# Stage four by sums and differences from batch 3 on, and a later exponential, in a prime-factor Fourier mixer with routed experts

## The chip, the cores and the metric

The kernel runs on one core of one Trainium2 chip. The metric is the device time of one execution in microseconds. The engines are named as the profile names them: PE (matrix products), PEld (its loads of the stationary operand), DVE (VectorE), ACT (ScalarE), POOL (GpSimd) and SP (SyncE, whose queue issues most DMAs).

## The reference

The first block multiplies the spectrum of each sequence with a filter; the second sends every token to one of eight experts.

```python
# x: (8, 2496, 256), filt: (1249, 256), N = 8 * 2496 tokens, E = 8, F = 1024
X = np.fft.rfft(x, axis=1)
y = np.fft.irfft(X * (filt_r + 1j * filt_i), n=2496, axis=1)
x = y.reshape(N, 256)
logits = x @ w_gate
expert_idx = np.argmax(logits, axis=1)
probs = np.exp(logits - logits.max(-1, keepdims=True))
probs /= probs.sum(-1, keepdims=True) + 1e-09
gate = probs[np.arange(N), expert_idx]
out[n] = gate[n] * (np.maximum(x[n] @ w1[e], 0) @ w2[e])     # e = expert_idx[n]
```

All data are float32. One expert per token, no token dropped.

## The kernel before

**The transform.** 2496 = 39 x 64, and a token is numbered by q (0 to 38) and t (0 to 63), so that the transform of length 2496 becomes one of 39 and one of 64. Because the input is real, 20 of the 39 frequencies are enough. A batch passes four stages on PE, each with a DRAM round trip between, except in batch 0: stage A (`stage_a`, L342) transforms over q, three values of t at a time: 3 x 39 = 117 rows in, 3 x 40 = 120 rows out, 20 frequencies as real and imaginary part. Stage B (`stage_b`, L356) transforms over t; DVE (in the first batches POOL too) multiplies with the filter (L363 to L372). Stage C (`stage_c`, L382) goes back over t and stores U (`ud`). **Stage four**, `stage_d`, goes back over q: 120 rows (3 t, 20 real and 20 imaginary parts each) times the table `tds` (120 x 117) give 117 rows of tokens, 3 t by 39 q. There are 22 columns of 3 t each; the last holds one t alone (63), so it has 40 rows in. They go in six chunks of four columns, the last chunk of two. `mm` on two columns at a time is L401 (120 rows, 512 output columns); in the last chunk it is L405, one column at a time, 120 rows and then 40.

**Around stage four.** `load_u` (L334) fetches a chunk of U into an input buffer `fin` (seven of them, shared with the other stages), by one DMA, two for the last chunk. `evac` copies a bank of PSUM to SBUF; the program decides by its own reckoning (`free`, `now`) whether DVE or ACT does it (L228). The result `yo` is the token rows themselves. `turn_y` transposes them (L476), `logits` multiplies by the gate's weights (L490: four groups of 32 output rows in one bank, one per pair of columns), `turn_logits` transposes back (L501). `route` then finds, for eight columns at a time, the expert and the gate: DVE instructions on small tiles, an exponential on ACT (L527), and the "rank product", two matmuls with a triangle and with ones (L548, L549), which count how many tokens of each expert come before. From it comes the row in a DRAM list by expert, and POOL writes each column's 117 token rows there by one indirect DMA (`scatter`, L617).

**The experts.** Tiles of 512, 256 or 128 rows of that list are read back (`rows_in`, L712), transposed (`turn_x`, L753, which first copies the token numbers to `idt`, L747), multiplied by the expert's w1 and w2, and written to the output by indirect DMAs that read `idt` (L860). Large tiles do the first product by a seven-product scheme of quarters (`hidden_by_quarters`, L796; sums on DVE, L800; relu on ACT, L804); others plainly (`hidden`, L837). The second product is `result` (L854).

**What sets the order.** The order on PE, DVE, ACT and SP is the order in which the Python program issues. A list of transform steps, each with a place in its slot (one slot per batch), a condition and a cost, is mixed with the steps of the experts: `share()` says how many microseconds of experts go with one of the transform; a step whose input has not been loaded, or whose landing time (`lands`) lies ahead, lets the experts go first. Side jobs (`sides`: routing, maps of tiles) are generators, advanced a few operations after each step. `free["v"]`, `free["s"]`, `free["p"]` are the program's reckoning of when DVE, ACT and POOL come free. In slot k stage four belongs to batch k - 1.

```python
            evac(yo[:, j:j + 2, :D], p[:TP, :].rearrange("p (i d) -> p i d", i=2), 512)
```

is L406, the end of stage four before: one copy of a bank for each pair of columns.

Of the kernel before, what the change touches and what calls it, by code (L numbers as in the profile page):

```python
# [19 lines left out]
P = 128  # L20
# [18 lines left out]

def token(q, t):  # L40
    return (q * N2 * pow(N2, -1, N1) + t * N1 * pow(N1, -1, N2)) % S


def coefficients():

    k = np.arange(S)
    of = np.zeros((N2, N1), int)
    of[k * pow(N1, -1, N2) % N2, k * pow(N2, -1, N1) % N1] = k
    return of[:, :NF]


def dft_tables():
# [27 lines left out]
    for j in range(NB):  # L80
# [6 lines left out]

    return {
# [6 lines left out]
        "valid": valid.reshape(TP, NG),  # L95
    }
# [22 lines left out]
def kernel(  # L119
# [13 lines left out]
    valid: bass.AP,  # L133
    out: bass.AP,
# [46 lines left out]

    tas = cst.tile([TP, TK], F32, name="tas")
    tbs = cst.tile([P, P], F32, name="tbs")
    tcs = cst.tile([P, P], F32, name="tcs")
    tds = cst.tile([TK, TP], F32, name="tds")
    sgs = cst.tile([P, NF // 2], F32, name="sgs")
# [5 lines left out]
    tri = cst.tile([TP, TP], F32, name="tri")  # L192
    ones = cst.tile([TP, P], F32, name="ones")
    segs = {w: cst.tile([P, E * w], F32, name=f"seg{w}") for w in (8, NG % 8)}
    ids0 = cst.tile([TP, NG], F32, name="ids0")
    vld = cst.tile([TP, NG], F32, name="vld")
# [63 lines left out]
    def load_rest():  # L260
        nc.sync.dma_start(out=tds, in_=td)
        nc.vector.memset(wg, 0.0)
        nc.sync.dma_start(out=wg[:, :, :E], in_=moe_w_gate.rearrange("(i p) e -> p i e", p=P))
        nc.sync.dma_start(out=ids0, in_=ids)
        nc.sync.dma_start(out=vld, in_=valid)

    def make_constants():
# [3 lines left out]
            out=tri, in_=ones[:, :TP], compare_op=ALU.is_gt, fill=0.0, base=0, pattern=[[1, TP]], channel_multiplier=-1  # L271
# [15 lines left out]
    def columns(ap, i0, n):  # L287
# [4 lines left out]
        if m < n:  # L292
            yield NS, slice(m, n), rows[(NG - 1) * TK:, :].rearrange("(i p) d -> p i d", p=NS)

# [35 lines left out]
    def load_u(b, c):  # L330
        i0, n = CH[c]
        ui = fin(("u", b, c))
        for r, m, v in columns(ud[b], i0, n):
            nc.sync.dma_start(out=ui[:r, m], in_=v)  # L334

    def stage_a(b, c):
        i0, n = CH[c]
        xt = ins.pop(("x", b, c))
        zo = sb.tile([TK, 4, D], F32, tag="st", name="zo", bufs=4)
        for j in range(0, n, 2):  # L340
            p = bank()
            mm(p[:TK, :], lhsT=tas, rhs=xt[:TP, j:j + 2, :], start=True, stop=True)  # L342
            evac(zo[:, j:j + 2, :], p[:TK, :].rearrange("p (t d) -> p t d", t=2), 512)
# [31 lines left out]
    def stage_c(b, f):  # L375
# [8 lines left out]
        if j == 2:  # L384
            f0 = f - 2
            move(ud[b][:, f0:f0 + 4, :], uo[:HP])
            move(ud[b][:, NF + f0:NF + f0 + 4, :], uo[HP:])
# [3 lines left out]
    def stage_d(b, c):  # L391
        if c == 0:
            lgs[b] = sb.tile([TP, NG, E], F32, tag="lg", name="lg")
# [3 lines left out]
        yo = outs["o", b, c] = sb.tile([P, 4, DR], F32, tag="y", name="yo", bufs=YB)[:TP]  # L397
        for j in range(0, n, 2):
            p = bank()
            if i0 + j + 2 < NG:  # L400
                mm(p[:TP, :], lhsT=tds, rhs=ui[:TK, j:j + 2, :], start=True, stop=True)  # L401
            else:

                for i, k in enumerate((TK, NS)):
                    mm(p[:TP, i * D:(i + 1) * D], lhsT=tds[:k, :], rhs=ui[:k, j + i, :], start=True, stop=True)  # L405
# [64 lines left out]
    def turn_y(b, c):  # L470
        yo = outs["o", b, c]
        for j in range(0, CH[c][1], 2):
            pt = bank().rearrange("p (i q) -> p i q", i=4)
            for i in range(2):
                for dh in range(DH):
                    nc.tensor.transpose(  # L476
                        pt[:, 2 * i + dh, :TP], yo[:, j + i, dh * P:(dh + 1) * P], ident[:TP, :TP]
                    )
            yt = yts[b, c, j] = sb.tile([P, 4, TP], F32, tag="yt", name="yt", bufs=4)
            evac(yt, pt[:, :, :TP], 4 * TP)  # L480

    def logits(b, g):
# [4 lines left out]
        lt = psr.tile([P, 2, E * NG], F32, tag="rk", name="lt")[:, :, :TP]  # L487
# [4 lines left out]
        ls = sb.tile([P, 2, TP], F32, tag="ls", name="ls", bufs=1)  # L492
# [3 lines left out]
    def turn_logits(b):  # L496
        g, w, ls = outs.pop(("l", b))
        n = w // CT
        pt = bank()[:TP, :2 * w].rearrange("p (i w) -> p i w", i=2)
# [8 lines left out]
    def route(b, g):  # L508
        t0 = 8 * g
        w = min(8, NG - t0)  # L510
        lg = lgs[b][:, t0:t0 + w]
        sh3 = (TP, w, E)
        she = (TP, E, w)

        def small(name, *shape, dt=F32, tag=None, rows=TP):
# [11 lines left out]
        nc.scalar.activation(ex, ex, AF.Exp)  # L527
        nc.vector.tensor_tensor(oh, oh, em8[:TP, None, :].to_broadcast(sh3), op=ALU.mult)
# [4 lines left out]
        nc.vector.tensor_tensor(idx, idx, vld[:, t0:t0 + w], op=ALU.mult)  # L533
# [3 lines left out]
            oe, idx[:, None, :].to_broadcast(she), em8[:TP, :, None].to_broadcast(she), op=ALU.is_equal  # L537
        )
        sd = small("sd", w)
        nc.vector.tensor_reduce(sd, ex, axis=AX.X, op=ALU.add)  # L540
        yield 2

        due = free["v"] + 1.0
        while now[0] < due:
            yield "wait"
        rk = psr.tile([P, 2, E * NG], F32, tag="rk", name="rk")
        oef = oe.rearrange("p e t -> p (e t)")
        mm(rk[:TP, 0, :E * w], lhsT=tri, rhs=oef, start=True, stop=True)  # L548
        mm(rk[:, 1, :E * w], lhsT=ones, rhs=oef, start=True, stop=True)  # L549
        rks = sb.tile([P, 2, 8 * E], F32, tag="rks", name="rks", bufs=1)  # L550
        nc.vector.tensor_copy(rks[:TP, 0, :E * w], rk[:TP, 0, :E * w])
        nc.vector.tensor_copy(rks[:, 1, :E * w], rk[:, 1, :E * w])
        nc.vector.tensor_scalar(sd, in0=sd, scalar1=1e-9, scalar2=None, op0=ALU.add)
        nc.vector.reciprocal(sd, sd)
        yield 4
        yos = [outs.pop(("o", b, c)) for c in range(2 * g, min(2 * g + 2, len(CH)))]
        for c, yo in enumerate(yos):
            n = min(4, w - 4 * c)
            sh8 = (TP, n, 8)
            nc.vector.tensor_scalar(  # L560
                yo.bitcast(I32)[:, :n, D:D + 8], in0=ids0[:, t0 + 4 * c:t0 + 4 * c + n, None].to_broadcast(sh8),
# [13 lines left out]
        nc.vector.tensor_tensor(posf, runf[:TP], rks[:TP, 1, :E * w], op=ALU.subtract)  # L575
        nc.vector.tensor_tensor(posf, posf, rks[:TP, 0, :E * w], op=ALU.add)
        yield 2
        bs = sb.tile([TP, E], F32, tag="bs", name="bs", bufs=1)
        nc.vector.tensor_tensor(bs, cnt[:TP], eoff[:TP], op=ALU.add)
# [6 lines left out]
        row = sb.tile([TP, 8], U32, tag="row", name="row", bufs=2)[:, :w]  # L586
        nc.vector.tensor_copy(row, rowf)  # L587
# [542 lines left out]
```

## Time and profile before

| | us |
|---|---|
| median of 8 runs (1547.03 to 1556.15) | 1552.12 |
| the profiled execution, its time | 1551.63 |
| its span, first to last instruction | 1549.9 |
| PE busy, whole span | 1503.69 |
| PE busy in stage four: L401, L405, 300 to 960 us | 47.26, 6.07 |
| DVE idle before L747, waiting for the output's DMAs | 141.1 |
| DVE idle before L540, waiting for the exponential | 18.4 |

A row of the profile names the line, the engine, the operation and the tiles, out <- in, with the shapes and how often it occurs; then the busy time, the mean of one in ns, the idle time of the engine just before, and what ended it. A float32 matmul is recorded twice, so 2 records are one `mm`. Matmuls overlap their neighbours, so their mean (594 ns for L401) is longer than the distance from one start to the next; the lists in order of time give that distance. The mean granted clock of the execution is 0.992.

### The profile page before, as it was taken

What the parts mean: (1) busy time and instruction counts of PE and PEld (TensorE: products, weight loads), DVE (VectorE), ACT (ScalarE), POOL (GpSimd) and SP (SyncE); (2) the same over time, 40 slices, a digit from 0 to 9 for tenths busy, and PEclk for the clock granted to TensorE, in tenths of its full rate; (3) what the DMA queues carried; (4) which work ended last, traced back from release to release, by engine and by line L of the source; (5) the groups of instructions that cost most, each with busy time, mean ns of one, the idle gap of its engine ahead of it and who ended that gap; (6) DMA issues with size and microseconds to landing.
All of it is one profiled execution on the core that took longest, in us unless ns stands there. A gap on an engine that the chain in (4) does not pass through costs nothing.

```text
span 1549.9 us, 23842 instructions
## 1 busy us (share of the span) xinstructions
PE 1503.7 (97%) x7524; PEld 1193.9 (77%) x7524; DVE 748.3 (48%) x1916; ACT 519.3 (34%) x1053; POOL 669.8 (43%) x814
## 2 busy tenths in 40 slices
PE   7998898999999999999999999999999999999998
PEld 6543454877678767788688788888888889999997
DVE  4676757434666555455755444675334333430000
ACT  3443433333333333233332333322222232224343
POOL 3322334313535445355356544573546455731111
PEclk9998999999999999999999999999999999999999
DMA  9759896885896387444844644435455433355551
GB/s 234 187 150 291 270 291 236 252 258 169 241 293 186 112 230 218 131 155 135 202 133 135 163 151 124 145 118 191 158 174 173 154 117 93 118 182 175 180 177 38
DMA packets 116160, 276.78 MB, mean 179 GB/s; under 512 B 17155, under 2 KB 58124, under 8 KB 116037
## 3 DMA queue, kind: packets, MB, share of 16 engines
q1 hardware_dynamic: 96917, 231.93, 50.6%
q0 software_dynamic: 19120, 43.33, 8.0%
q8 instruction: 63, 1.03, 0.3%
q14 instruction: 60, 0.49, 0.1%
HBM read 195.19 MB, written 80.64 MB: 178 GB/s over the span
## 4 chain that ended last, share of the span: by engine, by line
PE 76%; DMA 9%; issue 8%; DVE 5%; POOL 2%; ACT 0%; SPq 0%; POOLq 0%; DVEq 0%; ACTq 0%
PE bank L854 30%; PE bank L796 22%; DMA out_dram<-ys,idt 5%; PE bank L401 4%; PE bank L356 3%; PE bank L342 3%; PE bank L837 3%; PE bank L382 3%; PE bank L476 2%; PE bank L753 2%; PE lt L490 1%; DVE hT L800 1%; DMA ud<-uo 1%; DMA fin<-ud 1%; PE bank L423 1%
## 5 line engine op out<-in xcount | busy, mean ns | idle before, releaser
L854 PE MATMUL bank<-w2t,hT 128*128 128x256 f32 x1984 | 442.0, 380 | 0.1
L800 DVE TENSOR_TENSOR hT<-bank,hT 128x512 f32<-128x512 f32 (+1 forms) x504 | 299.4, 627 | 294.3 <-PE bank L796 190.4
L854 PEld LDWEIGHTS bank<-w2t,hT 128*128 128x128 f32 x1984 | 373.1, 190 | 63.7 <-issue 13.6
L860 POOL DMA_INDIRECT out_dram<-ys,idt x161 | 159.5, 991 | 503.8 <-ACT ys L859 239.7
L617 POOL DMA_INDIRECT rows<-yo,row x176 | 174.8, 993 | 174.0 <-DVE row L587 61.9
L804 ACT ACTIVATE hT<-hT 128x1024 f32<-128x1024 f32 (+1 forms) x144 | 133.2, 957 | 319.6 <-DVE hT L800 319.6
L859 ACT ACTIVATE ys<-bank,gts 128x256 f32<-128x256 f32 x156 | 73.7, 474 | 406.3 <-PE bank L854 351.8
L796 PE MATMUL bank<-xT,w1t 128*128 128x256 f32 (+1 forms) x864 | 190.3, 356 | 0.0
L796 PEld LDWEIGHTS bank<-xT,w1t 128*128 128x128 f32 x864 | 151.6, 190 | 21.9 <-issue 4.6
L796 PE MATMUL bank<-sums,wsum 128*128 128x256 f32 (+1 forms) x576 | 135.6, 358 | 0.3 <-POOL sums L760 0.3
L854 PE MATMUL bank<-w2s,hT 128*128 x592 | 132.9, 380 | 0.9 <-DVE hT L800 0.7
L837 PEld LDWEIGHTS bank<-xT,w1t 128*128 128x128 f32 x864 | 115.1, 192 | 14.2 <-issue 7.8
L837 PE MATMUL bank<-xT,w1t 128*128 128x128 f32 (+1 forms) x864 | 124.9, 300 | 0.6 <-DMA w1t<-in_moe_w_dram 0.6
L854 PEld LDWEIGHTS bank<-w2s,hT 128*128 128x128 f32 x592 | 110.2, 190 | 15.6 <-DVE hT L800 1.8
L796 PEld LDWEIGHTS bank<-sums,wsum 128*128 128x128 f32 x576 | 100.3, 190 | 20.3 <-issue 9.4
L771 POOL TENSOR_TENSOR wsum<-w1t 128x256 f32<-128x256 f32 x72 | 53.2, 738 | 105.8 <-PE bank L796 87.6
L363 DVE TENSOR_TENSOR ys<-bank,ht 128x512 f32<-128x512 f32 x80 | 54.9, 687 | 79.6 <-PE bank L356 79.0
L747 DVE COPY idt<-xg 128x4 int32<-128x4 int32 (+2 forms) x63 | 18.1, 287 | 149.0 <-DMA out_dram<-ys,idt 141.1
L843 ACT ACTIVATE hT<-bank 128x128 f32<-128x128 f32 (+1 forms) x214 | 63.6, 300 | 53.6 <-PE bank L837 48.3
L401 PE MATMUL bank<-fin,tds 120*117 120x512 f32 x140 | 70.0, 623 | 11.3 <-DMA fin<-ud 10.5
L382 PE MATMUL bank<-ys,tcs 128*128 128x512 f32 x140 | 73.0, 603 | 3.0 <-DVE ys L372 3.0
L342 PE MATMUL bank<-fin,tas 117*120 117x512 f32 x154 | 74.9, 604 | 0.6 <-ACT hT L809 0.4
(151 smaller groups left out, 1773.3 us busy)
## 6 DMA issues: line engine op xcount, KB each, us to landing
w1t<-in_moe_w_dram SPq DMA_DIRECT2D x126, 512.0 KB
w2t<-in_moe_w_dram SPq DMA_DIRECT2D x68, 512.0 KB
fin<-in_x_dram SPq DMA_DIRECT2D x39, 512.0 KB
fin<-zd SPq DMA_DIRECT2D x70, 256.0 KB
ud<-uo SPq DMA_DIRECT2D x70, 256.0 KB
zd<-zo SPq DMA_DIRECT2D x35, 480.0 KB
fin<-ud SPq DMA_DIRECT2D x35, 480.0 KB
xg<-rows SPq DMA_DIRECT2D x28, 544.0 KB
```

Source lines behind the costliest of these rows:

```text
L342: mm(p[:TK, :], lhsT=tas, rhs=xt[:TP, j:j + 2, :], start=True, stop=True)
L382: mm(p, lhsT=tcs, rhs=ys, start=True, stop=True)
L401: mm(p[:TP, :], lhsT=tds, rhs=ui[:TK, j:j + 2, :], start=True, stop=True)
L617: sc = nc.gpsimd.indirect_dma_start(out=rowsd, out_offset=bass.IndirectOffsetOnAxis(ap=at, axis=0), in_=what, in_offset=None,)
L796: mm(q[:, v], lhsT=left[:, v * P:(v + 1) * P], rhs=right, start=True, stop=True)
L800: nc.vector.tensor_tensor(o, q, a, op=ALU.add)
L804: nc.scalar.activation(o.rearrange("p v r c -> p v (r c)"), q.rearrange("p v r c -> p v (r c)"), AF.Relu)
L837: mm(p[:, :m], lhsT=w1t[2 * i + g][:, dh, fh, v * P:(v + 1) * P], rhs=xts[i][:, dh, :m], start=(dh == 0), stop=(dh == DH - 1))
L843: lambda: nc.scalar.activation(hT, p[:, :m], AF.Relu))
L854: mm(p[:, :D], lhsT=hs[i][k % 4 // 2][:, k // 4, k % 2, j * P:(j + 1) * P], rhs=w2, start=(k == 0), stop=(k == FT - 1))
L859: lambda: nc.scalar.activation(ys, p[:, :D], AF.Copy, scale=gate))
L860: nc.gpsimd.indirect_dma_start(out=out, out_offset=bass.IndirectOffsetOnAxis(ap=idt[i].bitcast(U32)[:, j, :], axis=0), in_=ys, in_offset=None,
```

## The change

For batches 3 to 7 (`SUMS_D = 3`) stage four uses that the cosine table is even and the sine table odd in q: with E the product of the cosines and the real parts and O that of the sines and the imaginary parts, token q is E + O and token 39 - q is E - O, for q = 0 to 19. The work of two old columns (6 t) is two halves of 3 t, r = 0 and 1; each half has 60 rows of real and 60 of imaginary parts. U is stored as a block of real and a block of imaginary parts. `load_u` brings for each chunk four pieces: the real parts of r = 0 to partitions 0 to 59 and of r = 1 to 64 to 123, the imaginary parts crosswise. Four matmuls of 60 rows and 64 output rows follow: E of r = 0 and of r = 1 into one bank, O of both into another. ACT copies O to SBUF, DVE writes the sum and the difference. A column of `yo` now has 124 rows; where a row is no token (four between the halves, q = 0 of the difference, t already done by the last column's neighbour) its row number is put past the end of the list, and the indirect DMA leaves it out by a bounds check, which all scatters now have. In the last chunk all four matmuls have 60 rows too, one column each.

Besides: the exponential of `route` is issued just before the rank product instead of three steps earlier, and the sum over it after the copies of the ranks, in all batches; `idt` has four buffers for three; the reckoned time of a relu starts when DVE is free, and that of the first sum in a quarter when ACT is; the cost of a chunk of stage four in the step list is 0.28 a column for 0.43 in the slots k > 3, which is from batch 3 on; `fill` is taken from another pool; two new tables replace the token numbers and the marks of valid rows after batch 2's routing, and a third (`tds2`) is loaded.

```diff
+    def other_tables():
+        nc.sync.dma_start(out=ids0, in_=ids2)
+        nc.sync.dma_start(out=vld, in_=valid2)
+        yield "wait"
+        nc.vector.tensor_scalar(off, in0=vld, scalar1=-float(TR), scalar2=float(TR), op0=ALU.mult, op1=ALU.add)
+        yield 1
...
+    def sum_columns(ap, i0, m):
+        rows = ap.rearrange("t s d -> (t s) d")
+        for k in range(2):
+            for r in range(2):
+                r0 = k * N2 * NF + NF * min(6 * i0 + 3 * r, N2 - 3)
+                at = 64 * (r ^ k)
+                if m == 2:
+                    v = rows[r0:r0 + 9 * NF].rearrange("(a p) d -> p a d", p=3 * NF)[:, 0:3:2]
+                else:
+                    v = rows[r0:r0 + 3 * NF, None, :]
+                yield slice(at, at + 3 * NF), slice(k * m, (k + 1) * m), v
...
+        if b >= SUMS_D:
+            for r, m, v in sum_columns(ud[b], 2 * c, n // 2):
+                nc.sync.dma_start(out=ui[r, m], in_=v)
+            return
...
-            move(ud[b][:, f0:f0 + 4, :], uo[:HP])
-            move(ud[b][:, NF + f0:NF + f0 + 4, :], uo[HP:])
+            re, im = by_f(ud[b], b >= SUMS_D)
+            move(re[:, f0:f0 + 4, :], uo[:HP])
+            move(im[:, f0:f0 + 4, :], uo[HP:])
...
+        if b >= SUMS_D:
+            m = n // 2
+            ps2 = [bank()[:, :m * D], bank()[:, :m * D]]
+            for k in range(2):
+                for r in range(2):
+                    g = 64 * (r ^ k)
+                    mm(ps2[k][64 * r:64 * r + 64], lhsT=tds2[g:g + 3 * NF, 64 * k:64 * k + 64],
+                       rhs=ui[g:g + 3 * NF, k * m:(k + 1) * m, :], start=True, stop=True)
+            pe, po = (p[:TR2].rearrange("p (i d) -> p i d", i=m) for p in ps2)
+            low, high = yo[:, :m, :D], yo[:, m:n, :D]
+            nc.scalar.copy(out=high, in_=po)
+            nc.vector.tensor_tensor(low, pe, high, op=ALU.add)
+            nc.vector.tensor_tensor(high, pe, high, op=ALU.subtract)
+            free["s"] = max(free["s"], now[0]) + 0.15 + 0.22 * m
+            free["v"] = max(free["v"], free["s"]) + 0.2 + 0.55 * m
+            lands["o", b, c] = free["v"] + 0.5
+            return
...
-        nc.scalar.activation(ex, ex, AF.Exp)
...
-        sd = small("sd", w)
-        nc.vector.tensor_reduce(sd, ex, axis=AX.X, op=ALU.add)
-        yield 2
+        yield 1
         due = free["v"] + 1.0
         while now[0] < due:
             yield "wait"
+        nc.scalar.activation(ex, ex, AF.Exp)
+        free["s"] = max(free["s"], now[0]) + 0.3
...
         nc.vector.tensor_copy(rks[:, 1, :E * w], rk[:, 1, :E * w])
+        sd = small("sd", w)
+        nc.vector.tensor_reduce(sd, ex, axis=AX.X, op=ALU.add)
...
-        nc.vector.tensor_copy(row, rowf)
+        if b >= SUMS_D:
+            nc.vector.tensor_tensor(row, rowf, off[:, t0:t0 + w], op=ALU.add)
+        else:
+            nc.vector.tensor_copy(row, rowf)
...
-            m = N1 if t0 + t == NG - 1 else TP
+            m = N1 if t0 + t == NG - 1 and b < SUMS_D else tp
...
+            bounds_check=TR - 1,
+            oob_is_err=False,
...
-        idt[i] = pools["moe"].tile([P, 4, 1], I32, tag="idt", name="idt", bufs=3)
+        idt[i] = pools["moe"].tile([P, 4, 1], I32, tag="idt", name="idt", bufs=4)
...
-            free["v"] = max(free["v"], now[0]) + 0.15 + 0.14 * n
+            free["v"] = max(free["v"], now[0], free["s"] if o is first else 0.0) + 0.15 + 0.14 * n
...
-            free["s"] = max(free["s"], now[0]) + 0.2 + 0.22 * n
+            free["s"] = max(free["s"], now[0], free["v"]) + 0.2 + 0.22 * n
...
-                    steps.append((at, lambda c=c: stage_d(k - 1, c), ("u", k - 1, c) if k > 1 else "y", 0.43 * CH[c][1]))
+                    steps.append((at, lambda c=c: stage_d(k - 1, c), ("u", k - 1, c) if k > 1 else "y",
+                                  (0.28 if k > SUMS_D else 0.43) * CH[c][1]))
...
-                    steps.append((at + 0.03, lambda c=c: turn_y(k - 1, c - 1), None, 0.22 * CH[c - 1][1]))
+                    steps.append((at + 0.03, lambda c=c: turn_y(k - 1, c - 1), ("o", k - 1, c - 1) if k > SUMS_D else None, 0.22 * CH[c - 1][1]))
```

## The prediction

> **What bounds the kernel.** I read the page's busy shares first, then the busy time by stretch, then PE's waits, then the order of PE's work around stage four. The profiled execution took 1551.63 us, its span is 1549.9; the median of the eight runs is 1552.12, 0.5 above the profiled one. I sum against 1551.63 and add 0.5 at the end.
>
> ```profile
> PE 1503.7 (97%) x7524; PEld 1193.9 (77%) x7524; DVE 748.3 (48%) x1916; ACT 519.3 (34%) x1053; POOL 669.8 (43%) x814
> ```
> ```profile
> 100.00:300.00 200.00, 176.63 (x691) 101.73 (x690) 128.44 (x390) 73.91 (x154) 72.08 (x75) 0.95 0.86 266
> 300.00:950.00 650.00, 646.37 (x3029) 498.41 (x3028) 358.80 (x904) 217.04 (x392) 301.55 (x357) 1.00 0.61 180
> ```
>
> The columns of a stretch are its length, then the busy time of PE, PEld, DVE, ACT, POOL, the granted clock, the DMA share and GB/s. Stage four of batches 3 to 7 (the only ones whose arithmetic changes) lies at 303 to 944 us. There PE is idle for 3.6 us in 650, at full clock. So in that stretch a microsecond of PE time saved or added is a microsecond of the run, until another engine makes PE wait; DVE is busy for 55% and ACT for 33%.
>
> **PE time of stage four now.** The order of PE's work (start, us, line, count) gives the price of a chunk by the distance between starts:
>
> ```profile
> 746.21 1.02 PE L382 MATMUL bank<-ys,tcs 128*128 128x512 f32 x2
> 747.07 1.88 PE L401 MATMUL bank<-fin,tds 120*117 120x512 f32 x4
> 748.79 3.62 PE L854 MATMUL bank<-w2t,hT 128*128 128x256 f32 x16
> ...
> 752.25 0.31 PE L548 MATMUL rk<-oe,tri 117*117 117x48 f32 x2
> ```
> ```profile
> 828.01 1.21 PE L405 MATMUL bank<-fin,tds 120*117 120x256 f32 x4
> 829.15 1.99 PE L796 MATMUL bank<-xT,w1t 128*128 128x256 f32 x8
> ```
>
> A matmul is two records. A chunk of four columns (two matmuls, four records) takes 748.79 - 747.07 = 1.72 us, 0.43 a record of 512 columns, and no gap before or after: 16 records of 256 columns behind it take 3.46 us, 0.216 each, half of 0.43. The last chunk (L405) has two matmuls of 120 rows and two of 40. It takes 1.14 us to the next start, and that work starts about 0.10 late, so 1.24, though its four records of 256 columns make 0.86. A batch: 5 x 1.72 + 1.24 = 9.84 us.
>
> **What replaces it.** Per chunk four matmuls of 60 rows and 64 output rows, each over half of the columns: two products by input half and output half, so that each uses one quarter of the array. The trace has no matmul pair on different input rows, but it has pairs on different output rows: the logits (L490), four of 32 output rows in turn.
>
> ```profile
> 785.85 0.41 PE L490 MATMUL lt<-yt,wg 128*32 128x234 f32 x4
> ```
> ```profile
> 914.81 3.62 PE L854 MATMUL bank<-w2t,hT 128*128 128x256 f32 x16
> 918.36 1.00 PE L490 MATMUL lt<-yt,wg 128*32 128x234 f32 x16
> 919.29 3.72 PE L854 MATMUL bank<-w2t,hT 128*128 128x256 f32 x16
> 922.85 0.96 PE L476 MATMUL bank<-ident,yo 117*128 117x117 f32 x8
> ```
>
> The first line is what PE has in flight in a hundredth of a microsecond at 785.90: four records at once. The second fence prices the group. From 914.81 to 922.85 are 8.04 us; the two L854 groups take 2 x 3.46 = 6.92, so the 16 records of L490 take 1.12. Four turns of 234 columns at 0.43 per 512 are 0.79. The rest, 0.34, is the way into the narrow form and out of it.
>
> If all four quarters run together, a chunk has two turns of 512 columns: 2 x 0.43 + 0.34 = 1.20 us; the last one two of 256: 0.43 + 0.34 = 0.77. A batch: 5 x 1.20 + 0.77 = 6.77, 3.07 less than 9.84. Five batches: **-15.3 us**.
>
> Both ends of this unknown: with no price for the way in and out, five batches save 5 x 6 x 0.34 = 10.2 us more; with all four one after another, a chunk is 4 x 0.86 + 0.34 = 3.78 and the last 2.06, 11.1 us a batch more, +56 in all. I take the value of the nearest row, L490.
>
> A page of the Trainium skill speaks against it. "TensorEngine Tiling (Array Packing)", section Restrictions and Gotchas, says that matmuls on different input rows cannot use one PSUM bank at the same time; here the first two products of a chunk do write one bank. By that rule the chunk would be the slower one of the second rival below. "PSUM — Partial Sum Buffer", section PSUM bank collisions, narrows it to the same bank and the same 32 partitions, which these two do not share; no row here decides between them.
>
> **What grows.** Tiles have 124 rows for 117. The transposes (L476, eight in 0.80 us, 0.10 each) stream 7 columns more of 117: at most 0.006 each, 44 a batch, 220 in all, +1.3. The logits stream 248 columns for 234: 14 x 0.43/512 = 0.012 a turn, 12 turns a batch, +0.7. Sum **+2.0**.
>
> **Beside PE**, and priced at nothing because of what hides it:
> - Emptying the banks. Now 42 ACT copies (0.586) and 13 DVE copies (0.689) in five batches; then 30 ACT copies (16 us for 24.3) and 60 DVE sums. By the row below (a DVE sum of a bank and a tile, 0.685), 50 x 0.69 + 10 x 0.38 = 38 us for 9.0: DVE goes from 359 to 388 us of 650. The cover is the 45% that DVE still has, and that other PE work is put between the products and their transposes, which wait until the sums are reckoned done. If it is gone, each chunk costs PE up to one late sum, 0.69.
> - Loads of U: four issues a chunk for one (two in the last), nearly the same bytes in the same 1 KB pieces. SP took 5.53 us for seven in the last batch; 24 at that mean are 19 us, at the median of 0.41 they are 10. The next w1 loads stand behind them. PE waited 0.4 us for a U load in the whole stretch; ends 0 and +4.
> - POOL's scatters get a bounds check and up to 124 rows: the other indirect writes (L860), checked and with 128 rows, take 991 ns, these (L617) 993. Nothing.
> - New tables: three small DMAs once. The two that overwrite the old ones wait on SP for the last routing of batch 2, and loads stand behind; ends 0 and +3, I take 0.
> - The exponential behind the wait for the rank product: DVE waited 18.4 us, four times, for it, and PE waited 3.8 us for what comes after in routing. ACT now has it later, where a relu that waits for DVE can stand before it. Ends -4 and +4, I take 0.
> - The fourth buffer of idt takes away DVE waits of 141.1 us, but only 9.5 of them before 960 us; after that DVE has little to do and PE is never idle. Nothing.
> - The program's reckoning of relu and sums changes which engine empties a bank, and the mixed order, in all batches. From 100 to 300 us PE is idle for 23 us, its longest single wait 5.2; ends -5 and +5, I take 0.
>
> ```profile
> L800 DVE TENSOR_TENSOR hT<-bank,hT 128x512 f32<-128x512 f32 x217 | 142.2, 685 | 81.6 <-PE bank L796 51.8 <-ACT hT L809 24.3
> ```
> ```profile
> 877.25 5.53 SPq L334 DMA_DIRECT2D fin<-ud  x7
> ```
>
> **Sum.** -15.3 + 2.0 = -13.3: 1551.63 - 13.3 + 0.5 = **1539 us**.
>
> **Rivals.**
> - The wait moves. PE is in order; a transpose whose sum is late stops all behind it, and the banks are held for three operations instead of one. For: ACT stands idle 149 us behind DVE's sums in this stretch, so a copy can be stuck behind a relu. Against: PE waited for DVE and ACT only 3.1 us in 650. If one chunk in three waits one sum, 10 x 0.69 = 7 us: 1546. From 13.3/30 = 0.44 us a chunk the gain is gone; this is also the case within 0.2%.
> - Slower: the quarters do not all run together. The queue order is upper-left, lower-right, then the two others. If matmuls on different input rows follow one another, while those on the same rows and other outputs go together as in L490, a chunk is three turns: 3 x 0.86 + 0.34 = 2.92, the last 1.63, a batch 16.2, +6.4; five, +32, and +2 of growth: 1586. If they pair, two turns: 2.06 and 1.20, a batch 11.5: +8.3 + 2.0, 1562. It decides from about 1.55 turns of 0.86 a chunk on. For: no row shows two input halves at once. Against: nothing in the code joins them, they read and write different partitions.
> - Better: the way in and out is cheaper for four wide quarters, or the order before 300 us comes out well: 1529.
>
> **Chances.** The forecast, 1533 to 1545: 0.58. Waits that eat part, 1545 to 1552: 0.12. Waits that eat more, up to 1560: 0.06. Quarters not together, 1562 to 1586 and above: 0.15. Better, below 1533: 0.09. A difference of 0.2% (3 us) is about what a measurement of this kernel can tell from no change. Faster by over that (below 1549): 0.58 + 0.09 + 0.08 of the waits = 0.75. Within: 0.04 + 0.03 = 0.07. Slower: 0.15 + 0.03 = 0.18. The range has the forecast, most of the better case and of the waits: 1529 to 1556, 0.80.
>
> **What would show it.** In the order of PE's work, the new line's eight records start four at a time within some hundredths, the next four 0.43 later, and the next line about 1.1 us behind the first; three or four steps would be the second rival. PE's idle time from 300 us to the end of stage four stays under 6 us; if it names DVE yo, DMA fin<-ud or w1t, the first rival holds. L476 and L490 grow by 6% a record. The tail after it is the same length and only starts earlier. I am wrong if the span changes by more before 300 us than in stage four.

## The result, and the profile after

The changed kernel takes 1558.54 us (median of 14 runs, 1555.65 to 1562.42) where the kernel before took 1550.32 in 40 runs. The ratio is 1.0057, interval 1.0045 to 1.0069: **8 us slower**, where 1539 was predicted. The profiled execution took 1561.77 us with a span of 1560.1. Line numbers moved: L487 is the new product of stage four, L492 ACT's copy, L493 and L494 DVE's sum and difference, L577 the transposes, L591 the logits, L722 the scatter, L903 / L907 / L911 the quarters with their sums and relus, L961 the second product.

The page's busy line and the busy time by stretch, to be laid beside those of before:

```profile
PE 1497.2 (96%) x7644; PEld 1180.0 (76%) x7644; DVE 815.1 (52%) x2041; ACT 481.9 (31%) x963; POOL 708.6 (45%) x815
```
```profile
100.00:300.00 200.00, 175.65 (x689) 103.86 (x688) 125.21 (x383) 72.20 (x147) 73.11 (x76) 0.94 0.84 265
300.00:950.00 650.00, 632.54 (x3115) 475.28 (x3114) 410.20 (x989) 193.31 (x348) 334.14 (x355) 1.00 0.61 179
```

PE has less to do, 1497.2 us for 1503.7, in a span that is 10.2 longer. From 100 to 300 us nothing moved (idle 24.4 us for 23.4). The time came in between 300 and 950 us: there PE now stands idle for 17.5 us of 650, before it was 3.6. DVE went from 358.8 to 410.2 us and POOL from 301.6 to 334.1.

What ended PE's idle time in that stretch (us in total, times, longest):

```profile
PE bank L438 <- DMA fin<-zd: 5.1, 1, 5.1
PE lt L591 <- DVE rks L652: 1.9, 3, 1.0
PE bank L961 <- PE bank L860: 1.8, 3, 0.8
PE bank L424 <- DMA fin<-in_x_dram: 1.7, 1, 1.7
PE bank L577 <- DVE hT L907: 1.4, 1, 1.4
PE bank L464 <- DVE yo L494: 1.2, 1, 1.2
```

No cause stands out. The longest is a load of stage B's input (`zd`), another the late difference (L494), most are other work that came late.

In most chunks the products run as forecast. In order of time around two chunks (start, us, line, count):

```profile
418.37 1.09 PE L487 MATMUL bank<-fin,tds 60*64 60x512 f32 x8
...
425.17 1.09 PE L487 MATMUL bank<-fin,tds 60*64 60x512 f32 x8
426.19 1.07 PE L577 MATMUL bank<-ident,yo 124*128 124x124 f32 x8
432.38 2.05 PE L438 MATMUL bank<-fin,tbs 128*128 128x512 f32 x2 [5.13 <-DMA fin<-zd]
434.22 1.79 PE L464 MATMUL bank<-ys,tcs 128*128 128x512 f32 x2
435.85 1.88 PE L424 MATMUL bank<-fin,tas 117*120 117x512 f32 x4
```

All eight records of a chunk are done in 1.09 us, and the next line starts 1.02 behind the first: all four quarters run together. In three places of 300 to 950 us they do not, at 563.7, 743.0 and 871.5 us. The first of them:

```profile
563.66 1.08 PE L487 MATMUL bank<-fin,tds 60*64 60x512 f32 x4
565.22 1.07 PE L487 MATMUL bank<-fin,tds 60*64 60x512 f32 x4 [0.49 <-ACT hT L916]
566.23 1.13 PE L903 MATMUL bank<-sums,wsum 128*128 128x256 f32 x4
```

The chunk takes 2.57 us for 1.02, because its second bank comes free only when ACT has emptied it (L916 is ACT's copy of a bank of the quarters). The three places cost 5.0 us together, of which the profile marks 1.2 as idle.

The last three lines of the list before show something else: after the wait of 5.13 us the pair L438, which otherwise takes 0.86 from start to start, takes 1.84, and L464 takes 1.63 for 0.86. The granted clock says why (columns as before; the clock stands third from the end):

```profile
425.00:432.30 7.30, 2.25 (x19) 1.16 (x18) 5.61 (x23) 2.16 (x5) 1.14 (x1) 1.00 0.99 291
432.30:436.00 3.70, 3.62 (x5) 1.64 (x6) 1.50 (x3) 0.00 (x0) 2.83 (x3) 0.54 1.01 302
```

A wait of 5.13 us was followed by 3.4 us at half clock, some 1.75 us more (0.98 on L438 and 0.77 on L464).

Where PE's time went from 300 us on, in us, from each record's start to the next with the idle time taken out (summed from the trace):

| | before | after | no sums (e1) | 128 rows (e3) | copies (e9) |
|---|---|---|---|---|---|
| stage four, batches 3 to 7 | 49.1 | 32.5 | 49.1 | 30.6 | 30.5 |
| transposes of its result | 22.1 | 24.7 | 22.2 | 25.2 | 24.9 |
| logits | 14.0 | 16.7 | 14.5 | 17.1 | 16.0 |
| stages A, B, C | 90.7 | 94.4 | 90.9 | 92.0 | 91.9 |
| idle, 300 to 950 us | 3.6 | 17.5 | 2.6 | 11.1 | 12.1 |

By these rows stage four gave 16.6 us. But the way into and out of the narrow form lengthens the records just before and after a chunk, which stand in other rows: 0.7 us before, 5.4 after. With it stage four gave 11.8 us (49.7 to 37.9). The transposes and logits took back 5.3, stages A to C 3.7 (1.75 of it the half clock above, 0.9 two records more behind 300 us), and the idle time 13.9.

### The profile page after: what moved, and what is told of

Its sections match the earlier page's. It is cut to its first block, busy times and chain, and to the rows that moved or that the text cites. A ratio compares the mean times of both kernels' runs of the same rounds, so it can differ in the third digit from the quotient of the medians.

```text
span 1560.1 us, 24416 instructions
## 1 busy us (share of the span) xinstructions
PE 1497.2 (96%) x7644; PEld 1180.0 (76%) x7644; DVE 815.1 (52%) x2041; ACT 481.9 (31%) x963; POOL 708.6 (45%) x815
## 3 DMA queue, kind: packets, MB, share of 16 engines
q0 software_dynamic: 28080, 43.49, 8.9%
## 4 chain that ended last, share of the span: by engine, by line
PE 81%; DMA 6%; DVE 6%; issue 4%; POOL 1%; ACT 1%; SPq 1%; POOLq 0%; DVEq 0%; ACTq 0%
PE bank L961 34%; PE bank L903 22%; PE bank L944 6%; PE bank L438 3%; PE bank L424 3%; PE bank L464 3%; PE bank L860 2%; PE bank L577 2%; PE bank L487 2%; DVE hT L907 1%; DMA ud<-uo 1%; DMA fin<-zd 1%; PE lt L591 1%; PE bank L502 1%; DMA fin<-in_x_dram 1%
## 5 line engine op out<-in xcount | busy, mean ns | idle before, releaser
L907 DVE TENSOR_TENSOR hT<-bank,hT 128x512 f32<-128x512 f32 (+1 forms) x504 | 300.1, 626 | 282.0 <-PE bank L903 190.7
L961 PE MATMUL bank<-w2t,hT 128*128 128x256 f32 x1984 | 442.6, 380 | 2.8 <-PE bank L860 1.8
L961 PEld LDWEIGHTS bank<-w2t,hT 128*128 128x128 f32 x1984 | 372.9, 190 | 70.6 <-issue 14.5
L722 POOL DMA_INDIRECT rows<-yo,row x176 | 212.6, 1208 | 179.0 <-issue 53.6
L911 ACT ACTIVATE hT<-hT 128x1024 f32<-128x1024 f32 (+1 forms) x144 | 133.2, 957 | 378.4 <-DVE hT L907 378.0
L903 PE MATMUL bank<-xT,w1t 128*128 128x256 f32 (+1 forms) x864 | 191.5, 358 | 0.9 <-POOL xT L869 0.9
L966 ACT ACTIVATE ys<-bank,gts 128x256 f32<-128x256 f32 x138 | 65.3, 473 | 406.9 <-PE bank L961 325.3
L903 PEld LDWEIGHTS bank<-xT,w1t 128*128 128x128 f32 x864 | 152.0, 191 | 25.9 <-issue 5.7
L903 PE MATMUL bank<-sums,wsum 128*128 128x256 f32 (+1 forms) x576 | 136.9, 360 | 3.2 <-POOL wsum L879 3.2
L961 PE MATMUL bank<-w2s,hT 128*128 x592 | 132.8, 379 | 1.2 <-DVE hT L907 1.2
L961 PEld LDWEIGHTS bank<-w2s,hT 128*128 128x128 f32 x592 | 110.2, 190 | 15.4 <-DVE hT L907 1.7
L903 PEld LDWEIGHTS bank<-sums,wsum 128*128 128x128 f32 x576 | 100.7, 191 | 25.5 <-issue 9.8
L438 PE MATMUL bank<-fin,tbs 128*128 128x512 f32 x140 | 74.3, 614 | 7.0 <-DMA fin<-zd 5.1
L464 PE MATMUL bank<-ys,tcs 128*128 128x512 f32 x140 | 74.2, 612 | 6.1 <-DVE ys L454 4.9
L273 DVE COPY xT<-bank 128x512 f32<-128x512 f32 (+2 forms) x88 | 42.9, 515 | 67.3 <-PE bank L860 67.3
```

What stands on the lines that cost most here:

```text
L438: mm(p, lhsT=tbs, rhs=zi[:, j:j + 2, :], start=True, stop=True)
L464: mm(p, lhsT=tcs, rhs=ys, start=True, stop=True)
L722: sc = nc.gpsimd.indirect_dma_start(out=rowsd, out_offset=bass.IndirectOffsetOnAxis(ap=at, axis=0), in_=what, in_offset=None, bounds_check ...
L903: mm(q[:, v], lhsT=left[:, v * P:(v + 1) * P], rhs=right, start=True, stop=True)
L907: nc.vector.tensor_tensor(o, q, a, op=ALU.add)
L911: nc.scalar.activation(o.rearrange("p v r c -> p v (r c)"), q.rearrange("p v r c -> p v (r c)"), AF.Relu)
```

## The experiments

All were timed in five rounds beside the kernel before in the same job: 1549.9 us in the job of e1 to e4, 1550.7 in e5 to e8, 1551.8 in e9 to e12, but 1566.6 in e13 to e16 and 1564.3 in e17 and e18. Ratios stand to the kernel before of their own job; how far those of two jobs can be compared is taken up at e18. The first theories were: A, the new reckoning of relu and sums disturbs the order; B, POOL's scatters; C, stage four's own new form, by its loads (C1) or by the chain of copy, sum and transpose (C2); D, that a shorter stage four leaves no cover for what feeds PE.

### Which part of the change: e1 to e4

e1, everything but the sums:

```diff
-SUMS_D = 3
+SUMS_D = 99
```

> The changed kernel with stage four as before in all batches: what is left of the change are the new reckoning of relus and first sums, the later exponential, the fourth idt buffer and the bounds check. Theory A (reckoning): the new reckoning sends copies from ACT to DVE, DVE is late and PE waits; then the loss stands here without the gain of stage four, 1562 to 1572 us. Theory B (scatter of 124 rows slow on POOL) and theory C (the chain of ACT copy and two DVE sums, and four loads a chunk on SP): within 4 us of the kernel before, 1546 to 1554.

Measured: 0.9995 (0.9978 to 1.0012), idle 2.6 us from 300 to 950. The exponential, `idt`, the reckoning and the bounds check are worth nothing together (the new tables are not loaded here). But it is not nothing for DVE, whose busy time is the third of the stretch, behind PE and PEld:

```profile
300.00:950.00 650.00, 647.45 (x3036) 498.86 (x3035) 382.97 (x950) 200.34 (x350) 304.53 (x361) 1.00 0.59 179
```

The reckoning alone moves bank copies from ACT to DVE: DVE has 383.0 us before a single sum is made.

e2, the sums without the rest (old reckoning, old place of the exponential, three `idt` buffers):

> Stage four by sums from batch 3 on, with the old reckoning, the old place of the exponential and three idt buffers. Theory A: the gain of stage four comes out, 1535 to 1543 us. B and C: no better than the changed kernel, 1555 to 1562.

Measured: 1.0075 (1.0052 to 1.0097). The loss is stage four's. DVE has 380.2 us of busy time from 300 to 950 us here, where after has 410.2: so how busy DVE is does not by itself explain the loss.

e3, columns of 128 rows for 124 (two small tiles of `route` share a buffer to make room):

```diff
-TR2 = 2 * (64 - 4) + 4
+TR2 = P
...
```

> The changed kernel with columns of 128 rows instead of 124 in batches 3 to 7 (four more rows that are no token; the place of two small tiles is shared to make room). If the scatters fall from 1.32 to the 0.99 us that the output's writes of 128 rows take, POOL loses some 36 us of work. Theory B: PE's waits go with it, 1540 to 1550 us. A and C: 1557 to 1561, the larger transposes cost about 1 us.

Measured: 1.0025 (1.0014 to 1.0037), some 5 us better than after. The scatters are what differs most; their row of before (117 rows), of after, and then of e3:

```profile
L617 POOL DMA_INDIRECT rows<-yo,row x176 | 174.8, 993 | 174.0 <-DVE row L587 61.9 <-issue 54.1 <-DVE cnt L588 30.5
```
```profile
L722 POOL DMA_INDIRECT rows<-yo,row x176 | 212.6, 1208 | 179.0 <-issue 53.6 <-ACT yo L273 40.2 <-DVE gts L855 22.4
```
```profile
L722 POOL DMA_INDIRECT rows<-yo,row x176 | 175.3, 996 | 188.2 <-issue 53.6 <-ACT yo L273 38.1 <-DVE cnt L693 26.4
```

Within after, those of batches 0 to 2 (117 rows, with the bounds check) take 986 ns (medians), those of batches 3 to 7 (124 rows) 1320. The bounds check is free; 124 rows cost 0.33 us each, 110 x 0.33 = 37 us of POOL, and 128 rows cost nothing. Idle time of PE falls from 17.5 to 11.1 us.

PE waits for POOL nowhere in this stretch, in after or in e3. What differs most is the load of `zd`: the 5.13 us before L438, 6.9 with the half clock behind it, are 1.0 in e3. e2 and e4, the other kernels with 124 rows, wait 4.3 and 2.3 us for `zd`, also between 418 and 428 us; no kernel with 128 rows waits longer than e3. So the slow scatters may delay this load; that they do is not shown.

e4, the change with the old reckoning:

```diff
-            free["v"] = max(free["v"], now[0], free["s"] if o is first else 0.0) + 0.15 + 0.14 * n
+            free["v"] = max(free["v"], now[0]) + 0.15 + 0.14 * n
...
-            free["s"] = max(free["s"], now[0], free["v"]) + 0.2 + 0.22 * n
+            free["s"] = max(free["s"], now[0]) + 0.2 + 0.22 * n
```

> The changed kernel with the old reckoning of relus and first sums alone. Theory A: 1536 to 1546 us. B and C: 1554 to 1562.

Measured: 1.0106 (1.0084 to 1.0127). Theory A falls: the old reckoning does not bring the gain back. DVE is busy for 382.4 us here, as in e2. By the ratios the new reckoning even helps, by some 7 us, but e2, with the old one too, lies only 2.8 us above after. From 300 to 950 us half clock costs e4 10.2 us and e2 3.4.

### The chain and the loads: e5 to e10

e5 is e1 with each U chunk of batches 3 to 7 in four DMAs:

```diff
+        if b >= 3:
+            for r, m, v in columns(ud[b], i0, n):
+                w, h = m.stop - m.start, r // 2
+                for a in (slice(0, h), slice(h, r)):
+                    for j in range(0, w, max(1, w // 2)):
+                        e = min(w, j + max(1, w // 2))
+                        nc.sync.dma_start(out=ui[a, m.start + j:m.start + e], in_=v[a, j:e])
+            return
```

> The kernel without sums (stage four as before), but from batch 3 on each chunk of U is fetched by four DMAs instead of one or two: two halves of the rows by two halves of the columns. Theory C1 (the 24 loads a batch hold SP, other loads land late): this alone costs 6 to 10 us on the kernel without sums, 1555 to 1559. Theory C2 (the chain of ACT copy and two DVE sums) expects nothing of it, 1546 to 1551.

Measured: 0.9976 (0.9963 to 0.9988), idle 2.9 us. The loads alone cost nothing beside the old stage four: C1 falls, as far as that goes (e14 and e17 come back to it).

e6 is e3 with two plain bank copies, so without sum and difference, and without the reckoned landing time:

```diff
-            nc.scalar.copy(out=high, in_=po)
-            nc.vector.tensor_tensor(low, pe, high, op=ALU.add)
-            nc.vector.tensor_tensor(high, pe, high, op=ALU.subtract)
...
+            evac(low, pe, m * D)
+            evac(high, po, m * D)
```

> The kernel with 128 rows, but stage four leaves out the sum and the difference: the two banks are copied as they are, each by the engine that the reckoning finds free. Products, loads, transposes and scatters are the same. C2: the gain of stage four comes out, 1536 to 1543 us. C1: as the kernel with 128 rows, 1550 to 1555.

Measured: 0.9982 (0.9968 to 0.9995), 0.0043 below e3, which ran in another job, and 4.8 us below e7, which ran in the same. Sum, difference and their chain cost some 5 to 7 us. What the chain looks like can be read from DVE's waits of after, from 300 to 950 us:

```profile
DVE yo L493 <- ACT yo L492: 56.1, 20, 9.9
```

In 20 of 30 chunks DVE stood before its sum until ACT had copied O. The row looks like a backlog of ACT, but most of it is none. Laid beside the ends of the products (as the trace models them) and the starts of the copies, 39.2 of the 56.1 us passed before the products were done: DVE was ahead of PE. 10.8 are the copy itself, and only 6.1 are ACT coming late. Of the longest, 9.9 us, 9.2 are of the first kind. The backlog shows at the other end: in 10 of 30 chunks the sum starts more than 2 us after the products' end, up to 12.2. In seven of these DVE was still busy with earlier work, in three the copy was late: ACT stands behind relus that wait for DVE's sums of the quarters (in the timeline a relu starts at 745.16 us after 8.08 us `<-DVE hT`). The banks are held meanwhile.

e7 is e3 with the transposes reckoned to be possible 3 us later:

```diff
-            lands["o", b, c] = free["v"] + 0.5
+            lands["o", b, c] = free["v"] + 3.5
```

> The kernel with 128 rows, with the transposes of a summed chunk held back 3 us longer, so that more of the experts' work stands between. If PE's waits come from transposes that stand too close behind the sums (C2 in its simplest form): 1542 to 1549 us. If DVE's load or the loads are the cause: 1551 to 1556.

Measured: 1.0017 (1.0005 to 1.0029): no difference from e3 that can be told. So it is not that the transposes come too early.

e8 is e3 with ACT writing -2 O, DVE the sum, and POOL the difference as sum minus 2 O:

```diff
+            nc.scalar.activation(high, po, AF.Copy, scale=-2.0)
+            nc.vector.scalar_tensor_tensor(out=low, in0=high, scalar=-0.5, in1=pe, op0=ALU.mult, op1=ALU.add)
+            nc.gpsimd.tensor_tensor(high, low, high, op=ALU.add)
...
```

> The kernel with 128 rows, with the difference moved to POOL: ACT copies minus twice the second product, DVE adds half of it back to the first, POOL adds both. DVE loses 30 operations of 0.65 us, and both banks come free one DVE operation earlier; POOL gains 30 of about 1.3. If DVE's load and the held banks are the cause: 1544 to 1550 us. If the loads are: 1551 to 1557.

Measured: 0.9992 (0.9979 to 1.0005), the best with the new stage four whole, though level with before. Two of its waits are now POOL's (`PE bank L578 <- POOL yo L494`, 5.4 us in all).

e9 is e6 with the landing time kept:

```diff
+            lands["o", b, c] = max(free["v"], free["s"]) + 0.5
```

> As the kernel with plain copies (128 rows, no sum and no difference), but the transposes still wait until the copies are reckoned done. If DVE's sums and their chain are what is left of the loss (theory C2): 1537 to 1544 us. If the rest comes from elsewhere (theory D: any change of the costs gives another order of work, and the order of the kernel before has fewer waits than most): 1547 to 1553.

Measured: 0.9985 (0.9974 to 0.9995). As e6, in another job: even with no sum to wait for, 12.1 us of idle time stay.

```profile
300.00:950.00 650.00, 637.86 (x3150) 483.63 (x3150) 389.12 (x963) 200.25 (x357) 304.77 (x361) 0.99 0.58 180
```

DVE and POOL are back near where e1 has them (383.0 and 304.5), so it is neither engine's load. No single wait explains it: the largest rows are loads of `w2t` (2.5 us), and the second bank of a chunk comes late in two places, for some 3 us in all (in e3 and e6 too, in e12 below not at all).

e10 is e1, the old products, with a chain like the new one, a DVE maximum of the bank and its copy, for which the transposes wait as well:

```diff
+            if b >= 3:
+                o = yo[:, j:j + 2, :D]
+                nc.vector.tensor_tensor(o, p[:TP, :].rearrange("p (i d) -> p i d", i=2), o, op=ALU.max)
+                free["v"] = max(free["v"], free["s"]) + 0.1 + 0.55
+                lands["o", b, c] = free["v"] + 0.5
...
```

> The kernel without sums, with the chain of the sums laid on the old stage four: from batch 3 on, after each copy of a bank, DVE takes the maximum of bank and copy (the same numbers), so 11 more DVE operations a batch that hold the bank, and the transposes wait for them. C2: the chain costs by itself 6 to 12 us, 1554 to 1561. If the chain hurts only where PE's time has become short: 1548 to 1552.

Measured: 1.0012 (1.0000 to 1.0023), against 0.9995: the chain alone costs some 2.6 us, at the edge of what the intervals can tell. DVE waits for ACT here as well, 43.5 us, while PE's idle time is only 5.6: such a wait is no measure of the cost.

```profile
DVE yo L510 <- ACT yo L273: 43.5, 25, 7.7
```

### Order: e11, e12, e15, e16

`RESERVE` is the reckoned time of expert work held back for the end; changing it changes only how the same work is mixed. e11 is e1, e12 is e8, e15 and e16 are e3:

```diff
-    RESERVE = 60.0
+    RESERVE = 50.0
```

> The kernel without sums, with the reserve of experts' work kept for the end at 50 us instead of 60: another mixed order, nothing else. Theory D: differs by more than 4 us from the kernel without sums, most likely slower. Otherwise within 3 us of 1548.6.

Measured: 0.9992 (0.9980 to 1.0005), as e1.

> The kernel with the difference on POOL, with a reserve of 50 us instead of 60. Theory D: differs by more than 4 us from 1549.3, either way. Otherwise within 3 us.

Measured: 1.0094 (1.0075 to 1.0113), where e8 had 0.9992. The same work in another order is 16 us longer. The two ran in different jobs; e6 and e9, nearly the same kernel, agree across these two jobs (0.9982 and 0.9985), so the job is an unlikely cause, though it is not excluded. PE's largest waits, 300 to 950 us, of e12 and then of e8:

```profile
PE bank L962 <- DMA w2t<-in_moe_w_dram: 7.7, 2, 6.2
PE bank L962 <- issue: 5.2, 1, 5.2
PE bank L578 <- POOL yo L494: 3.1, 1, 3.1
```
```profile
PE bank L578 <- POOL yo L494: 5.4, 2, 4.0
PE lt L592 <- DVE rks L653: 3.1, 1, 3.1
```

And its stretch, at a granted clock of 0.98:

```profile
300.00:950.00 650.00, 623.88 (x3064) 469.27 (x3063) 390.78 (x946) 190.27 (x336) 332.66 (x381) 0.98 0.57 176
```

PE's idle time is 26.1 us, and the clock's records hold three stretches at half speed that cost 11.9 us; e8 has 14.4 and 3.4 us. e1 and before have 2.6 and 3.6 us of idle time and no half clock. In e12 the three stretches begin behind or within waits of 6.2 us, of 2.1 and 5.2, and of 2.1 us. A wait of 3.1 us at 883 us was followed by none, and in e7 one of 1.8 us by 3.4 us at half clock. So a wait can cost itself and 1.7 us or more again, but its length alone doesn't tell whether it does.

e15 has 70, e16 has 50:

> The kernel with sums and 128 rows (1.0025), with the constant that holds work back for the end set to 70 instead of 60: the same work in another order. Theory 'order': with a short stage four the time hangs on the order that the planner happens on, so the two other settings (70 here, 50 in the run beside it) spread by 0.6% or more, and one may show the gain (0.992). Theory 'no order helps': both 1.001 to 1.005, idle in 300 to 950 us near 11 us.

> The same kernel with 50 instead of 60. Theory 'order': away from 1.0025 by 0.3% or more, as the kernel with the difference on GpSimd went from 0.9992 to 1.0094 at 50. Theory 'no order helps': 1.001 to 1.005.

Measured: 1.0073 (1.0052 to 1.0094) and 1.0109 (1.0085 to 1.0132), idle 23.0 and 24.1 us. No order gained. Within this one job the two orders lie 8 us apart (1576.55 and 1584.41), though the intervals of their ratios just overlap. How far they are from e3 isn't told: this job's kernel before took 1566.6 us, e3 wasn't in it, and e18 below shows that the ratio of such a kernel can move by 1.5% between jobs.

### A shorter stage four of the old kind: e13, e14, e17, e18

e13 is e1 with half of the old products left out: both evacuations read one bank.

```diff
         for j in range(0, n, 2):
+            if b >= 3 and j:
+                evac(yo[:, j:j + 2, :D], p[:TP, :].rearrange("p (i d) -> p i d", i=2), 512)
+                continue
             p = bank()
```

> The kernel without sums (0.9995), with one half of stage four's products left out from batch 3 on: of each chunk of four columns only the first two are computed, and both evacuations read that one bank. Part of the computation is left out. Old loads, old row count, no sums, no new products; TensorE has 25 groups of about 0.86 us less, 21 us. Theory 'cover': what feeds TensorE between 300 and 950 us sets the time, and any TensorE work taken away there comes back as waits: ratio 0.995 to 1.001, idle of TensorE in that stretch from 2.6 us up to 12 or more. Theory 'content': the new stage four brings a wait with it and a shorter one of the old kind would gain: ratio 0.985 to 0.990, idle under 6 us.

Measured: 0.9873 (0.9844 to 0.9901), 20 us off for 21 us of products. The theory that any shortening is lost falls by its time. Its idle time, 12.0 us, is what that theory had said; but with no e1 in this job, how much of it was there without the cut is not known.

e14 is e6 with one DMA for each chunk of U, which brings the wrong rows:

```diff
-            for r, m, v in sum_columns(ud[b], 2 * c, n // 2):
-                nc.sync.dma_start(out=ui[r, m], in_=v)
+            rows = ud[b].rearrange("t s d -> (t s) d")[160 * c:160 * c + n * TR2]
+            nc.sync.dma_start(out=ui[:, :n], in_=rows.rearrange("(p j) d -> p j d", j=n))
```

> The kernel with 128 rows and plain copies (0.9982), with each chunk of U loaded by one DMA of 128 whole stretches instead of four DMAs of rows of 1 KB; the rows it loads are not the right ones, so the result is left wrong, and sum and difference are left out as well. Theory 'loads with a short stage four': the loads cost nothing beside the old stage four (0.9976) only because that one was long; then idle of TensorE in 300 to 950 us falls from 12.7 to under 6 us and the ratio to 0.988 to 0.992. Theory 'cover': the idle time stays over 10 us, ratio 0.996 to 1.000.

Measured: 1.0124 (1.0099 to 1.0149), idle 28.2 us. Neither number was in a theory. One load a chunk brings no gain: e18, with four, has 1.0128, though in another job.

e17 is e5 with the edit of e13:

> The kernel with half of stage four's old products left out from batch 3 on (0.9873 on its chip), and each chunk of U loaded by four DMAs instead of two, 128 loads more on SyncE's queue; part of the computation is left out. Theory 'loads with a short stage four': the four loads take the gain back only once stage four is short: 0.996 or more. Theory 'form': the loss is in the new form of the products (128 rows, two banks held by each chunk, longer transposes), and loads cost nothing here either: 0.984 to 0.990.

Measured: 0.9865 (0.9841 to 0.9888). Four loads a chunk cost nothing beside a short stage four either.

e18 is e6 again, unchanged, in the job of e17:

> The kernel with 128 rows and plain copies once more (0.9982 before; it leaves out sum and difference), on the same chip as the run beside it. Theory 'form': 0.996 to 1.000 again, 0.8% or more above the run beside it. Theory 'chip': the gain of the kernel with half the products was the chip's, whose times of the kernel before stood 1% higher; then both runs here lie within 0.4% of each other.

Measured: 1.0128 (1.0101 to 1.0156), where the same kernel had 0.9982 in its first job. In the same job e17 and e18 have 27.7 and 30.6 us of stage four and differ by 41 us. Their stretches, e17 and then e18:

```profile
300.00:950.00 650.00, 636.93 (x3004) 495.33 (x3003) 385.70 (x958) 200.37 (x357) 306.42 (x363) 0.99 0.59 181
```
```profile
300.00:950.00 650.00, 622.71 (x2994) 466.78 (x2993) 377.47 (x918) 194.47 (x347) 288.97 (x343) 0.98 0.57 175
```

PE stands 13.1 and 27.3 us idle, and has two and six stretches of half clock (3.4 and 13.7 us). So "chip" alone doesn't explain it, and the loads don't: the form of the new stage four is in it. What of the form, the two banks that a chunk holds at once, the 128 rows, or the order that its cost of 0.28 a column gives, is not separated; e17 also keeps the old cost in the step list and takes one bank fewer a chunk.

## Why the prediction was wrong, point by point

**The removed products: right in price, not in what they wait for.** -15.3 was priced, with the way in and out. Counted so, -11.8 was measured, and -13.7 in e3. The rival that the quarters do not run together is out: with both banks free the chunk takes 1.22 us with its way in and out (1.20 was priced from L490). What is missing are the three places where the second bank was late: 3.8 us in stage four's row, beside 1.2 of idle time. The rule of the Trainium skill in "TensorEngine Tiling (Array Packing)", section Restrictions and Gotchas, does not hold for these two products on different input rows into one bank; their records start 7 ns apart, all four quarters within 20, as the narrower wording in "PSUM — Partial Sum Buffer", section PSUM bank collisions, allows (same bank and same 32 partitions).

**What grows: too small.** +2.0 was priced, +5.3 measured (transposes 2.6, logits 2.7). The streams grow by 6% as priced; where the rest comes from was not looked into.

**Scatters, "Nothing": wrong.** The rows of 117 and of 128 agreed within 2 ns, and 124 lay between; it costs 1320. Worth some 5 us (after against e3), which is about what the wait for `zd` and its half clock differ by.

**Emptying the banks: the step that failed.** "DVE goes from 359 to 388 us of 650. The cover is the 45% that DVE still has." The sums' own share was right: 27 us were added (e1's 383 to 410), 29 priced. The other 24 came from the reckoning, which was looked at for the order alone, and they are not the cost: e2 and e4 have 380 and 382 us and are no faster. What failed is the cover. A share of idle time is none where the work comes in a fixed order and a bank stays full until its turn: the sum started up to 12.2 us after its products. That the full bank is how this reaches PE is a reading of the trace; what the runs show is the price: some 5 to 7 us (e6 against e7 and e3), 2.6 where the old products got the same chain (e10).

**The first rival, "The wait moves", is what happened, but at another price.** It named DVE's `yo` and one late sum in every third chunk, 7 us in all. The sign set for it, idle time over 6 us from 300 us on, came: 17.5. `yo` is named for 1.6 of it, loads of z and x for 6.8, the routing for 2.8. The wait did not move to one place; the slack went out of many.

**The sum of the loss.** By ratios: some 5 us for the rows, some 6 for sums and chain, 3 for the growth that was too small. What then remains shows in e9: with the ways in and out its stage four has 14.2 us less than e1's and its transposes and logits some 4 more, so it should lie 10 us below e1; it lies 1.5 below, across two jobs. Some 8 us of gain are lost with neither sums nor slow scatters. In the profiles, from 300 to 950 us, e9 has 9.5 us more of idle time than e1, and half clock that costs 3.4 us where e1 has none. The prediction's "a microsecond of PE time saved or added is a microsecond of the run, until another engine makes PE wait" came to its "until" at once. Excluded, by the runs: the loads (e5, e17), the reckoning (e2, e4), the early transposes (e7), and a general rule that a shorter stage four gains nothing (e13, e17). What the runs suggest is that with the new form the time hangs on order (e12 against e8, 16 us across jobs; e15 against e16, 8 us within one) where without it it doesn't (e11 against e1). Which property of the form makes the order fragile **stays open**.

**Small terms: right.** Exponential, `idt`, reckoning and bounds check are together 0.9995 (e1), and before 300 us nothing moved. The new tables were not measured by themselves.

## What to carry to other kernels

A bottleneck engine that is idle for 0.5% of a stretch tells that time taken from it is gained only as long as every other engine's order keeps up; the share of idle time on the others doesn't tell that. Price a copy followed by a sum on two in-order engines by how long the bank stays full (here up to 12.2 us), not by the duration of the sum, and don't take an engine's own wait for a cost: most of DVE's 56 us were spent ahead of PE. Ask also for the moment at which all banks of a step are free, when it takes two at once for one after the other. And when rows of two sizes cost the same, try the very size that lies between: 124 rows cost a third more than 117 or 128.

## What the runs showed of the hardware that was not expected

- An indirect write of 124 rows took 1320 ns (median), one of 117 rows 986, one of 128 rows 988 to 996 (means), the bounds check nothing. In after 28080 packets went over the software queue, in before 19120.
- Half clock comes in multiples of 3.41 us. Between 300 and 950 us there is one such piece in after, behind the wait of 5.13 us, seven in three places in e12, eight in six places in e18, and none in before. The Trainium skill, "TensorE: Matmul & The Clock Gate", Part 1, gives a window of 3413 ns for it; the trace agrees.
- The same kernel took 1548.9 us in one job and 1586.1 in another, while the kernel before went from 1550.7 to 1564.3 only. In the slower jobs VectorE stood still where the profile names neither an instruction nor a DMA that it waits for. In e18, from 300 to 950 us:

```profile
DVE yo L273 <- issue: 8.3, 2, 4.5
DVE hT L903 <- issue: 6.4, 3, 5.2
DVE ys L445 <- issue: 4.9, 1, 4.9
```

e6, the same kernel in the earlier job, has no such wait in the whole span, after has 0.2 us, none of e1 to e12 over 2.0, and the six kernels of the later jobs have 20 to 34 (`issue` and `remote` together). What these stops are, the runs don't say; a PE wait of 4.2 us for `oe` is new in e18 beside them. e13 and e17 have 27 and 20 us of them and still lie at 0.987: beside the old products, halved, they did little harm.
